# Probabilities of an attention kernel by pairs of key tiles, in instructions of 768 columns

## The chip, the cores and the metric

The kernel runs on one core of one Trainium2 chip. The metric is the time of one execution on the device, in microseconds. Three runs of the kernel before took 981.05, 981.09 and 982.55 us; their median is 981.09 us.

## The reference

Block-sparse attention of 4 batches x 8 heads, 768 positions, 64 columns a head, followed by a two-layer network on the 3072 tokens. All inputs are float32.

```
scores = q @ k^T / sqrt(64);  scores = -1e9 outside the block mask
attn   = softmax(scores);     attn_out = attn @ v
x = attn_out as [3072, 512];  h = x @ w_in                 # 512 -> 2048
g = h where h >= 1, 0 where h <= -1, else (h + 1)^2 / 4
out = g @ w_out                                            # 2048 -> 512
```

## The kernel before

**Heads.** A head is worked through in two halves of 384 queries (`HALF`), and a half in six key tiles of 128 (`T`), so a head has 12 steps. In a step, TensorE (PE) makes the scores of one key tile, keys on the 128 partitions and queries on the 384 columns, by two matmuls into a PSUM bank (`scores`, L318 and L319). ScalarE (ACT) takes the exponential out of the bank into SBUF (`expo`, L323, tile `pt`). The row maximum that the exponent needs is made ahead of the head: twelve matmuls (`max_mm`, L267), each read by a maximum on VectorE (DVE) (`max_red`, L272, tile `mc`). Scores, maxima and small jobs share one ring of three PSUM banks, `pa`.

**Split and whole heads.** Heads 0 to 9 (`WHOLE` names pairs of heads) use the float32 probabilities as they are. For the other 22 heads the probabilities are split into a rounded part and the rest, both in the format that TensorE takes faster: `p_hi` (L196 through the helper `rounded`, a cast on ScalarE, tile `ph`), `p_lo` (L331, a subtraction of two SBUF tiles on VectorE, tile `pl`). Two matmuls a key tile then multiply them with the values (`values`, L350 and L351, bank `po`). `pt`, `ph` and `pl` have three buffers each, of 384 columns.

**Sums of the softmax.** In split heads, GpSimd (POOL) adds up the six `pt` tiles of a half (`p_sum`, L338, five adds of 384 columns, tile `acc`). VectorE then sums over the partitions with a transposing reduction (`acc_sum`, L373, tile `psum`), and after the second head of a pair TensorE, VectorE and some DMAs finish the reciprocal (`sums` L378, `dens`, `recip`, `r_out`), with which `x_mul`, `x_hi` and `x_lo` make the network's input `x`.

**The network.** It runs one batch behind the heads, in slices of 128 hidden columns, one slice in three steps. TensorE makes the slice by twelve matmuls into the one bank `hp` (`l1`, L472 to L474). ScalarE takes relu and square (L478, L481), VectorE merges them with `hp` (`g_max`, L484, tile `r`) and so frees the bank for the next slice. Then follow a cast `gh` on ScalarE, a subtraction `gl` on VectorE (L493), and nine matmuls of 512 columns (`l2`, L500 to L502, banks `oa`). In the first half of batch 0's network, ScalarE and VectorE also convert `w_out` from float64 (L168 to L180).

**The order.** Every step is put into `plan` with a due time in steps (`at`), from tables of numbers (`P`, `PW`, `PA`, `PM`): a split tile's cast is due 1.22 steps behind its scores, its low part 1.349, its add 0.841, its values `lag` = 3.5. The network of batch b begins at step 96 (b + 1) + `DELAY`. The plan is sorted by due time and issued; a scheduler below it may still place an instruction ahead of others of its engine. Each engine then works strictly in its order, and waits where an input or a buffer isn't there.

Of the kernel before, what the change touches and what calls it, by code (L numbers as in the profile page):

```python
# [8 lines left out]
F32 = mybir.dt.float32  # L9
F32R = mybir.dt.float32r  # L10
# [3 lines left out]
ALU = mybir.AluOpType  # L14
# [23 lines left out]
def body(ctx, tc, qk_t, v, sampled_blocks, moe_w_in, moe_w_out, ind, cm, negd, ident, fold, out):  # L38
    nc = tc.nc
    pool = lambda name, bufs, **kw: ctx.enter_context(tc.tile_pool(name=name, bufs=bufs, **kw))  # L40
# [2 lines left out]
    tp = pool("tp", 1)  # L43
    qk = pool("qk", SETS)
    vp = pool("vp", 2)
    pp = pool("pp", 3)
    ac = pool("ac", 2)
    pr = pool("pr", 1)
    xp = pool("xp", 10)
# [1 line left out]
    op = pool("op", 1)  # L51
# [21 lines left out]
    def f(ap):  # L73
        return ap.bitcast(F32)
# [12 lines left out]
    def consts():  # L87
        M = slice(64, KM)
        for i in range(SETS):
            nc.gpsimd.memset(f(QA[i][64:128]), 0.0)  # L90
        nc.gpsimd.memset(VW[0][:, :, 64:128], 1.0)
        nc.gpsimd.memset(VW[1][:, :, 0:64], 1.0)
        nc.vector.memset(eps, 1e-9)
        nc.vector.memset(half_c, 0.5)
        sraw = cst.tile([128, NR, 2], I32, name="sraw")
        nc.sync.dma_start(out=sraw[M], in_=sampled_blocks.bitcast(I32).rearrange("a (r w) -> a r w", w=2))
        cmt = cst.tile([128, 2 * NB], F32, name="cmt")
        nc.sync.dma_start(out=cmt[M], in_=cm)
        ef = f(cv.tile([128, 512, 2], I32, name="raw", bufs=3).rearrange("p c w -> p (c w)"))[64:KA, 0:S]
        nc.sync.dma_start(out=ef, in_=ind)  # L100
        idf = pp.tile([128, HALF], F32, name="pt")[:, 0:128]
        nc.sync.dma_start(out=idf, in_=ident)
        nc.vector.tensor_copy(out=idr, in_=idf)
        nc.vector.tensor_copy(out=KAt[0][64:KA], in_=ef)
        nc.sync.dma_start(out=nd, in_=negd.rearrange("a (t p) -> a t p", t=T))
        nc.sync.dma_start(out=sel, in_=fold)
        for i in range(1, SETS):
            rounded(nc.gpsimd, KAt[i][64:KA], ef)
        sf = cst.tile([128, NR], F32, name="sf")
        nc.vector.tensor_copy(out=sf[M], in_=sraw[M, :, 0])  # L110
        al = cst.tile([128, NB], F32, name="al")
        nc.vector.tensor_copy(out=al[M], in_=cmt[M, 0:NB])
        for r in range(NR):
            nc.vector.scalar_tensor_tensor(
                out=al[M], in0=cmt[M, NB:2 * NB], scalar=sf[M, r:r + 1], in1=al[M],
                op0=ALU.is_equal, op1=ALU.max)
        mb = cst.tile([128, NB], F32R, name="mb")
        nc.vector.tensor_scalar(out=mb[M], in0=al[M], scalar1=-1.0, scalar2=BIG, op0=ALU.add, op1=ALU.mult)
        for hf in range(2):
            cs = slice(hf * HALF, (hf + 1) * HALF)  # L120
            pm = psa.tile([128, 512], F32, name="pa")
            nc.tensor.matmul(out=pm[0:NB, 0:HALF], lhsT=mb[M], rhs=KAt[0][64:KM, cs], start=True, stop=True)
            for i in range(SETS):
                (nc.scalar.copy if i else nc.vector.tensor_copy)(out=QA[i][64:KM, cs], in_=pm[0:NB, 0:HALF])
# [4 lines left out]
    def at(t, fn, *args):  # L129
        plan.append((t, fn, args))  # L130
# [59 lines left out]
    def rounded(eng, dst, src):  # L190
        if eng is nc.vector:
            eng.tensor_copy(out=dst, in_=src)
        elif eng is nc.gpsimd:
            eng.tensor_scalar(out=dst, in0=src, scalar1=1.0, scalar2=0.0, op0=ALU.mult, op1=ALU.add)
        else:
            eng.copy(out=dst, in_=src)  # L196

    def head(i, n0, b, h, pst):

        j, e = divmod(h, 2)  # L200
        wide = i < H
        whole = i // 2 in WHOLE
# [116 lines left out]
            nc.tensor.matmul(out=ps[:, 0:HALF], lhsT=st["KB"][:, ks], rhs=st["QB"][:, cs], start=False, stop=True)  # L319

        def expo(c):
            p = st["p", c] = pp.tile([128, HALF], F32, name=("pt", "ph", "pl")[c % 3] if wide else "pt")
            nc.scalar.activation(out=p, in_=st.pop(("ps", c))[:, 0:HALF], func=AF.Exp, scale=SCALE)  # L323
# [5 lines left out]
        def p_lo(c):
            pl = st["pl", c] = pp.tile([128, HALF], F32R, name="pl")  # L330
            (nc.gpsimd if i < 2 * H and c in PL1 else nc.vector).tensor_tensor(out=pl, in0=st["p", c], in1=f(st["ph", c]), op=ALU.subtract)  # L331

        def p_sum(hf, c):
            if c == 1:
                st["acc", hf] = ac.tile([128, HALF], F32, name="acc")
            if c:
                prev = st["p", 0] if c == 1 else st["acc", hf]
                nc.gpsimd.tensor_tensor(out=st["acc", hf], in0=prev, in1=st["p", c], op=ALU.add)  # L338

        def values(hf, c):  # L340
            if c == 0:
# [71 lines left out]
        for hf in range(2):  # L413
            for c in range(T):
                at(s, scores, hf, c)
                at(s + G["ex"], expo, c)
                if not whole:
                    at(s + G["ph"], p_hi, c)
                    at(s + G["pl"], p_lo, c)
                    at(s + G["ps"], p_sum, hf, c)  # L420
                at(s + G["lag"], values, hf, c)
                s += 1
            u = s - 1 + G["lag"]
            if whole:
                at(u + G["ow"], o_whole, hf)
            else:
                at(u + G["ot"], o_tmp)
                at(u + G["oa"], o_add, hf)
                at(u + G["al"], acc_sum, hf)
                if e:  # L430
                    at(u + G["su"], sums, hf)
                    at(u + G["de"], dens, hf)
            if e:
                y = u + (G["yw"] if whole else G["yy"])
                if whole:
                    at(y, r_in, hf)
# [144 lines left out]
PA = {'vw': 4.0, 'r1': 0.857, 'r2': 4.031, 'qs': 11.825, 'vs': 8.565, 'ld': 5, 'm0': 7.832, 'm1': 5.139, 'mr': 0.063, 'mc': 2.3, 'mt': 1.564, 'mw': 0.515, 'ex': 0.037, 'ph': 1.22, 'pl': 1.388, 'ps': 0.841, 'ow': 0.331, 'ot': 0.188, 'oa': 0.814, 'ah': 0.068, 'al': 0.538, 'su': 0.644, 'de': 1.414, 'yw': 0.799, 'yy': 1.698, 'xm': 0.186, 'xh': 1.352, 'xl': 3.084, 'lag': 3.5}  # L581
PM = {'gr': 0.039, 'gs': 0.186, 'gm': 0.351, 'gh': 0.912, 'gl': 1.158, 'l2': 1.494, 'l3': 0.158, 'l1': 0.131}
RINGS = {"s": ("oa0", "oa1", "hp"), "m": ("pa", "pa")}
DELAY = 3.672
EARLY = 0
SETS = 2
MANUAL = -999
# [56 lines left out]
```

## Time and profile before

| | |
|---|---|
| median of three runs | 981.09 us |
| profiled execution, its time | 980.94 us |
| its span, first to last instruction | 979.0 us |
| granted TensorE clock, mean | 0.995 |
| TensorE matmuls busy | 945.3 us, 97% |
| VectorE busy | 736.8 us, 75% |
| ScalarE busy | 646.3 us, 66% |
| GpSimd busy | 251.5 us, 26% |

A row of instructions in a timeline gives start, duration, engine, line and tiles, and in brackets the idle time of its engine before it and who ended it. A group's row gives the count, the busy time, the mean duration in ns, and the idle time before. In a row of a line's own view stand the shortest, the median and the longest duration. Matmuls overlap, so their rate is read from start to start. Heads 10 to 31, the split ones, run from about 205 to 835 us; after them the last batch's network runs alone.

### The profile page before, as it was taken

Reading aid. Unit: us, or ns where it says so; the run is one execution under the profiler, and the core shown is the slowest. Engines: PE = TensorE matmul, PEld = TensorE weight load, DVE = VectorE, ACT = ScalarE, POOL = GpSimd, SP = SyncE. Lnnn points to the kernel's source line nnn. Section 1 sums busy time; section 2 is a strip of 40 time slices with the busy share of each in tenths; the row PEclk is TensorE's granted clock in tenths of the full one; section 3 lists DMA queues with packets and bytes.
Section 4 is the critical chain, followed back from the end, with each engine's and each line's share of the span. In section 5 each row is a group of like instructions: output and inputs, shape, how many; then the busy total and the mean of one; then the engine's idle time right before and its main releaser. Section 6 shows DMA issues by size and latency. Waiting matters only on the chain.

```text
span 979.0 us, 14671 instructions
## 1 busy us (share of the span) xinstructions
PE 945.3 (97%) x4746; PEld 833.3 (85%) x4746; DVE 736.8 (75%) x1390; ACT 646.3 (66%) x1326; POOL 251.5 (26%) x229
## 2 busy tenths in 40 slices
PE   5898999999899999999999999999999999999998
PEld 3676677888789999998999899999999999899997
DVE  5897988779998888988888888888788885422222
ACT  4686787677677676767677667776767676433433
POOL 1000000013334443433434343433434343000000
PEclk9899999999999999999999999999999999999999
DMA  6756766754364544545556453646445442433442
GB/s 193 227 155 183 200 201 214 259 173 140 129 205 144 146 148 136 178 135 154 158 154 189 118 153 120 198 138 176 137 143 178 126 114 89 154 129 129 161 129 97
DMA packets 56216, 154.44 MB, mean 158 GB/s; under 512 B 9612, under 2 KB 17952, under 8 KB 56140
## 3 DMA queue, kind: packets, MB, share of 16 engines
q1 hardware_dynamic: 56100, 153.48, 52.0%
q8 instruction: 38, 0.62, 0.3%
q14 instruction: 38, 0.31, 0.1%
q10 hardware_dynamic: 40, 0.03, 0.0%
HBM read 100.92 MB, written 14.81 MB: 118 GB/s over the span
## 4 chain that ended last, share of the span: by engine, by line
PE 88%; DVE 5%; ACT 3%; DMA 2%; issue 2%; SPq 0%; ACTq 0%; DVEq 0%
PE oa L500 8%; PE oa L502 8%; PE oa L501 8%; PE hp L472 8%; PE hp L474 8%; PE hp L473 8%; PE pa L267 7%; PE pa L318 5%; PE pa L319 5%; PE po L350 5%; PE po L348 5%; PE po L351 4%; PE oa L348 3%; DVE mc L272 1%; PE oa L318 1%
## 5 line engine op out<-in xcount | busy, mean ns | idle before, releaser
L338 POOL TENSOR_TENSOR acc<-acc,pt 128x384 f32<-128x384 f32 x176 | 202.2, 1149 | 226.2 <-ACT pt L323 190.3
L272 DVE TENSOR_REDUCE mc<-pa 128x1 f32<-128x384 f32 x384 | 202.8, 548 | 24.1 <-PE pa L267 21.0
L196 ACT CAST ph<-pt 128x384 fp32r<-128x384 f32 x264 | 135.7, 514 | 88.2 <-PE po L350 84.5
L331 DVE TENSOR_TENSOR pl<-pt,ph 128x384 fp32r<-128x384 f32 x264 | 166.3, 630 | 35.6 <-ACT ph L196 34.9
L323 ACT ACTIVATE pt<-pa 128x384 f32<-128x384 f32 x288 | 140.6, 489 | 50.8 <-PE pa L319 42.0
L472 PE MATMUL hp<-x,wi 128*128 128x384 f32 x448 | 155.0, 346 | 2.9 <-DVE r L484 2.9
L500 PE MATMUL oa<-w,gh 128*128 128x512 f32 x384 | 153.6, 400 | 0.3 <-ACT gh L196 0.3
L502 PE MATMUL oa<-w,gl 128*128 128x512 f32 x384 | 151.4, 394 | 0.0
L473 PE MATMUL hp<-x,wi 128*128 128x384 f32 x448 | 151.4, 338 | 0.0
L474 PE MATMUL hp<-x,wi 128*128 128x384 f32 x448 | 151.2, 338 | 0.0
L501 PE MATMUL oa<-w,gh 128*128 128x512 f32 x384 | 150.8, 393 | 0.0
L267 PE MATMUL pa<-KA,QA 88*128 88x384 f32 x384 | 138.8, 381 | 5.3 <-DMA QA<-qkh 3.0
L338 POOL TENSOR_TENSOR acc<-pt 128x384 f32<-128x384 f32 x44 | 45.8, 1040 | 349.4 <-ACT pt L323 349.4
L484 DVE SCALAR_TENSOR_TENSOR r<-r,hp 128x384 f32<-128x384 f32 x112 | 61.7, 551 | 74.0 <-ACT r L481 73.6
L493 DVE TENSOR_TENSOR gl<-r,gh 128x384 fp32r<-128x384 f32 x128 | 83.7, 654 | 23.4 <-ACT gh L196 22.9
L478 ACT ACTIVATE r<-hp,half_c 128x384 f32<-128x384 f32 x112 | 65.1, 582 | 53.4 <-PE hp L474 50.3
L318 PE MATMUL pa<-QA,KA 102*128 102x384 f32 x288 | 99.3, 345 | 0.8 <-ACT pt L323 0.4
L319 PE MATMUL pa<-QB,KB 128*128 128x384 f32 x288 | 97.9, 340 | 0.0
L267 PEld LDWEIGHTS pa<-KA,QA 88*128 88x128 f32 x384 | 73.2, 192 | 27.8 <-DVE mc L272 6.7
L350 PE MATMUL po<-ph,vn 128*128 128x384 f32 x264 | 91.5, 347 | 2.3 <-DVE xun L360 1.9
L472 PEld LDWEIGHTS hp<-x,wi 128*128 128x128 f32 x448 | 84.5, 189 | 8.6 <-DVE r L484 4.2
L351 PE MATMUL po<-pl,vn 128*128 128x384 f32 x264 | 88.6, 336 | 0.0
(100 smaller groups left out, 1634.1 us busy)
## 6 DMA issues: line engine op xcount, KB each, us to landing
w<-wo_dram SPq DMA_DIRECT2D x112, 512.0 KB
qk<-in_qk_t_dram SPq DMA_DIRECT2D x32, 384.0 KB
raw<-in_moe_w_in_dram SPq DMA_DIRECT2D x16, 512.0 KB
raw<-in_moe_w_out_dram SPq DMA_DIRECT2D x16, 512.0 KB
wo_dram<-w SPq DMA_DIRECT2D x16, 512.0 KB
lv<-in_v_dram SPq DMA_DIRECT2D x32, 192.0 KB
KA<-qkh SPq DMA_DIRECT2D x32, 192.0 KB
QA<-qkh SPq DMA_DIRECT2D x32, 192.0 KB
```

The lines of the kernel that those rows point to most:

```text
L267: nc.tensor.matmul(out=pm[:, 0:HALF], lhsT=QAi[0:KM, t * 128:(t + 1) * 128], rhs=KAi[0:KM, kh * HALF:(kh + 1) * HALF], start=True, stop=True)
L272: nc.vector.reduce_max(out=st["mc"][:, t, kh:kh + 1], in_=st.pop(("pm", t, kh))[:, 0:HALF], axis=AX.X)
L318: nc.tensor.matmul(out=ps[:, 0:HALF], lhsT=KAi[0:KA, ks], rhs=QAi[0:KA, cs], start=True, stop=False)
L319: nc.tensor.matmul(out=ps[:, 0:HALF], lhsT=st["KB"][:, ks], rhs=st["QB"][:, cs], start=False, stop=True)
L331: (nc.gpsimd if i < 2 * H and c in PL1 else nc.vector).tensor_tensor(out=pl, in0=st["p", c], in1=f(st["ph", c]), op=ALU.subtract)
L338: nc.gpsimd.tensor_tensor(out=st["acc", hf], in0=prev, in1=st["p", c], op=ALU.add)
L472: nc.tensor.matmul(out=hv, lhsT=wi[:, j, 0, fs], rhs=x[:, 0], start=(j == 0), stop=False)
L473: nc.tensor.matmul(out=hv, lhsT=wi[:, j, 0, fs], rhs=x[:, 1], start=False, stop=False)
L474: nc.tensor.matmul(out=hv, lhsT=wi[:, j, 1, fs], rhs=x[:, 0], start=False, stop=(j == NP - 1))
L500: nc.tensor.matmul(out=o, lhsT=gh[:, ts], rhs=w[:, 0], start=(fi == 0), stop=False)
L501: nc.tensor.matmul(out=o, lhsT=gh[:, ts], rhs=w[:, 1], start=False, stop=False)
L502: nc.tensor.matmul(out=o, lhsT=gl[:, ts], rhs=w[:, 0], start=False, stop=(fi == NF - 1))
```

## The change

The probabilities of two neighbouring key tiles (a pair, `cp`) now lie in one tile of 2 x 384 columns. The exponentials still come one by one, each into its half. In split heads, one cast, one low part and one add work on 768 columns. The add of pair 1 takes pairs 0 and 1, that of pair 2 adds to it, and a last add of 384 columns folds the two halves of `acc` together. `ph` and `pl` have two buffers of 768 columns, `pt` three. The values of split heads stand 4.0 steps behind their scores instead of 3.5, so that they stand right ahead of the scores of four tiles later, and the network's begin moves by the same half step.

```diff
-    pp = pool("pp", 3)
+    pp = pool("pp", 2)
...
         def expo(c):
-            p = st["p", c] = pp.tile([128, HALF], F32, name=("pt", "ph", "pl")[c % 3] if wide else "pt")
+            cp, k = divmod(c, 2)
+            if k == 0:
+                st["pp", cp] = pp.tile([128, 2, HALF], F32, name=("pt", "ph", "pl")[cp] if wide else "pt",
+                                         bufs=2 if wide and cp else 3)
+            p = st["p", c] = st["pp", cp][:, k]
...
-        def p_hi(c):
-            ph = st["ph", c] = pp.tile([128, HALF], F32R, name="ph")
-            rounded(nc.vector if c in (PH1 if i < 2 * H else PH2) else nc.scalar, ph, st["p", c])
...
+        def p_hi(cp):
+            ph = st["php", cp] = pp.tile([128, 2, HALF], F32R, name="ph")
+            rounded(nc.scalar, ph, st["pp", cp])
+            st["ph", 2 * cp], st["ph", 2 * cp + 1] = ph[:, 0], ph[:, 1]
+
+        def p_lo(cp):
+            pl = pp.tile([128, 2, HALF], F32R, name="pl")
+            nc.vector.tensor_tensor(out=pl, in0=st["pp", cp], in1=f(st["php", cp]), op=ALU.subtract)
+            st["pl", 2 * cp], st["pl", 2 * cp + 1] = pl[:, 0], pl[:, 1]
+
+        def p_sum(hf, cp):
+            if cp == 0:
+                return
+            if cp == 1:
+                st["acc2", hf] = ac.tile([128, 2, HALF], F32, name="acc")
+            acc = st["acc2", hf]
+            nc.gpsimd.tensor_tensor(out=acc, in0=st["pp", 0] if cp == 1 else acc, in1=st["pp", cp], op=ALU.add)
+            if cp == 2:
+                nc.gpsimd.tensor_tensor(out=acc[:, 0], in0=acc[:, 0], in1=acc[:, 1], op=ALU.add)
+                st["acc", hf] = acc[:, 0]
...
-                if not whole:
-                    at(s + G["ph"], p_hi, c)
-                    at(s + G["pl"], p_lo, c)
-                    at(s + G["ps"], p_sum, hf, c)
-                at(s + G["lag"], values, hf, c)
+                if not whole and c % 2:
+                    at(s + G["ph"] - 0.5, p_hi, c // 2)
+                    at(s + G["pl"] - 0.5, p_lo, c // 2)
+                    at(s + G["ps"], p_sum, hf, c // 2)
+                at(s + (G["lag"] if whole else LAG), values, hf, c)
                 s += 1
-            u = s - 1 + G["lag"]
+            u = s - 1 + (G["lag"] if whole else LAG)
...
+LAG = 4.0
...
-DELAY = 3.672
+DELAY = 4.172
```

In the changed file these lines move down: the casts keep L196, the maxima L272, the scores L318 and L319, but the exponential is L327, the low part L336, the add L345, the fold L347, the values L360 and L361, psum L383, the first layer L482 to L484, r L494, gl L503, the second layer L510 to L512.

The instructions come to stand in another order. Three places are shown, two of VectorE and one of TensorE. The first is on VectorE, at the end of a head's second half, before (numbers behind a name tell buffers apart; r reads and frees `hp`, psum reads `acc`):

```order
L331 TENSOR_TENSOR pl_7345<-pt_7321,ph_7341 128x384
L484 SCALAR_TENSOR_TENSOR r_7343<-r_7343,hp_7292 128x384
L331 TENSOR_TENSOR pl_7367<-pt_7351,ph_7365 128x384
L373 TENSOR_REDUCE psum_7086<-acc_7231 128x12
L493 TENSOR_TENSOR gl_7369<-r_7343,gh_7363 128x384
L331 TENSOR_TENSOR pl_7389<-pt_7373,ph_7387 128x384
```

The same place on VectorE now:

```order
L336 TENSOR_TENSOR pl_6761<-pt_6720,ph_6757 128x768
L298 TENSOR_TENSOR QA0_113<-pa_6787,nd_109 6x768
L336 TENSOR_TENSOR pl_6816<-pt_6782,ph_6810 128x768
L383 TENSOR_REDUCE psum_6577<-acc_6759 128x12
L494 SCALAR_TENSOR_TENSOR r_6812<-r_6812,hp_6773 128x384
L503 TENSOR_TENSOR gl_6835<-r_6812,gh_6833 128x384
```

r stood ahead of the half's last low part and of psum; it now stands behind both. Of the 44 psums of the program, 21 stand so: those of all second halves from the third split head on, and that of the last head's first half. The second place is the end of a first half in every other head (heads 13, 15 and so on to 29, nine in all), while the next head's row maxima are made. VectorE had there before:

```order
L331 TENSOR_TENSOR pl_7157<-pt_7135,ph_7153 128x384
L272 TENSOR_REDUCE mc_7123<-pa_7147 128x1
L484 SCALAR_TENSOR_TENSOR r_7155<-r_7155,hp_7108 128x384
L272 TENSOR_REDUCE mc_7123<-pa_7159 128x1
L373 TENSOR_REDUCE psum_6924<-acc_7047 128x12
L272 TENSOR_REDUCE mc_7123<-pa_7171 128x1
```

and has now:

```order
L336 TENSOR_TENSOR pl_6650<-pt_6613,ph_6642 128x768
L272 TENSOR_REDUCE mc_6604<-pa_6646 128x1
L383 TENSOR_REDUCE psum_6435<-acc_6590 128x12
L494 SCALAR_TENSOR_TENSOR r_6644<-r_6644,hp_6607 128x384
L272 TENSOR_REDUCE mc_6604<-pa_6663 128x1
L272 TENSOR_REDUCE mc_6604<-pa_6673 128x1
```

Here r has come to stand behind psum, and two maxima behind both. The third place is TensorE's order at the end of the second half, up to the next slice's first matmul into `hp`; before, from the sixth row behind the half's last score matmul on:

```order
L500 MATMUL oa1_6190<-w_7112,gh_7274 128x512
L501 MATMUL oa1_6190<-w_7112,gh_7274 128x512
L502 MATMUL oa1_6190<-w_7112,gl_7285 128x512
L318 MATMUL pa_7357<-QA0_113,KA0_115 128x384
L319 MATMUL pa_7357<-QB_7105,KB_7104 128x384
L500 MATMUL oa2_6209<-w_7112,gh_7274 128x512
L501 MATMUL oa2_6209<-w_7112,gh_7274 128x512
L502 MATMUL oa2_6209<-w_7112,gl_7285 128x512
L350 MATMUL po_7287<-ph_7312,vn_6719 128x384
L351 MATMUL po_7287<-pl_7314,vn_6719 128x384
L472 MATMUL hp_7375<-x_2531,wi_119 128x384
```

and now the last twelve rows of the same stretch:

```order
L319 MATMUL pa_6822<-QB_6585,KB_6584 128x384
L510 MATMUL oa1_5772<-w_6611,gh_6751 128x512
L511 MATMUL oa1_5772<-w_6611,gh_6751 128x512
L512 MATMUL oa1_5772<-w_6611,gl_6765 128x512
L510 MATMUL oa2_5788<-w_6611,gh_6751 128x512
L511 MATMUL oa2_5788<-w_6611,gh_6751 128x512
L512 MATMUL oa2_5788<-w_6611,gl_6765 128x512
L360 MATMUL po_6767<-ph_6757,vn_6231 128x384
L361 MATMUL po_6767<-pl_6761,vn_6231 128x384
L318 MATMUL pa_6839<-QA0_113,KA0_115 128x384
L319 MATMUL pa_6839<-QB_6585,KB_6584 128x384
L482 MATMUL hp_6842<-x_2438,wi_119 128x384
```

The values now stand right ahead of the scores. Counted from the half's last score matmul (L319, itself counted) to L482 there are now 12 matmuls of 384 columns and 9 of 512: ahead of these rows stand that L319, the last three of `l1`, three of `l2`, two of the values and L318.

More of the change, by code (lines that the diff above doesn't have):

```diff
@@ L100, in consts @@
         nc.sync.dma_start(out=ef, in_=ind)
-        idf = pp.tile([128, HALF], F32, name="pt")[:, 0:128]
+        idf = pp.tile([128, 2, HALF], F32, name="pt", bufs=3)[:, 0, 0:128]
         nc.sync.dma_start(out=idf, in_=ident)
@@ L321, in expo @@
         def expo(c):
-            p = st["p", c] = pp.tile([128, HALF], F32, name=("pt", "ph", "pl")[c % 3] if wide else "pt")
-            nc.scalar.activation(out=p, in_=st.pop(("ps", c))[:, 0:HALF], func=AF.Exp, scale=SCALE)
-        def p_hi(c):
-            ph = st["ph", c] = pp.tile([128, HALF], F32R, name="ph")
-            rounded(nc.vector if c in (PH1 if i < 2 * H else PH2) else nc.scalar, ph, st["p", c])
[L329 to L338, printed above, removed]
+            cp, k = divmod(c, 2)
[3 more added lines that the diff above has]
+            p = st["p", c] = st["pp", cp][:, k]
+            nc.scalar.activation(out=p, in_=st.pop(("ps", c))[:, 0:HALF], func=AF.Exp, scale=SCALE)
+        def p_hi(cp):
[16 more added lines that the diff above has]
+                st["acc", hf] = acc[:, 0]
         def values(hf, c):
```

## The prediction

> **What bounds the kernel now.** I read the page's busy times first, then the stretches, then who made TensorE wait.
>
> ```profile
> span 979.0 us, 14671 instructions
> PE 945.3 (97%) x4746; PEld 833.3 (85%) x4746; DVE 736.8 (75%) x1390; ACT 646.3 (66%) x1326; POOL 251.5 (26%) x229
> ```
>
> The stretches from 200 to 800 us hold nearly all the heads that the change touches; columns are PE, PEld, DVE, ACT, POOL busy.
>
> ```profile
> 200.00:250.00 50.00, 46.67 (x236) 40.31 (x237) 44.50 (x76) 37.57 (x78) 15.96 (x14) 1.00 0.53 172
> 250.00:300.00 50.00, 46.07 (x238) 40.43 (x237) 48.99 (x90) 34.05 (x72) 18.58 (x16) 1.00 0.47 156
> 300.00:800.00 500.00, 497.55 (x2618) 458.27 (x2617) 419.33 (x785) 355.71 (x743) 198.96 (x178) 1.00 0.52 152
> ```
>
> PE idles 3.33 + 3.93 + 2.45 = 9.7 us in these 600. So PE sets the pace, and the most that any relief of the other engines can return here is 9.7 us; 7.3 of it lies in 200 to 300 us, where VectorE is 93.5% busy (84% later). The waits of PE in 200 to 800 us:
>
> ```profile
> PE hp L472 <- DVE r L484: 2.9, 2, 2.0
> PE po L350 <- DVE xun L360: 1.9, 3, 0.9
> PE pa L267 <- ACT pt L323: 1.2, 3, 0.5
> PE po L350 <- ACT xun L368: 0.4, 1, 0.4
> ```
>
> That PE is really at its rate is seen in the starts, not in the overlapping spans:
>
> ```profile
> 560.48 0.33 PE L350 MATMUL po<-ph,vn 128*128 128x384 f32 x1
> 560.65 0.34 PE L351 MATMUL po<-pl,vn 128*128 128x384 f32 x1
> 560.83 0.39 PE L500 MATMUL oa<-w,gh 128*128 128x512 f32 x1
> 561.06 0.40 PE L501 MATMUL oa<-w,gh 128*128 128x512 f32 x1
> 561.29 0.39 PE L502 MATMUL oa<-w,gl 128*128 128x512 f32 x1
> 561.52 0.34 PE L318 MATMUL pa<-QA,KA 102*128 102x384 f32 x1
> ```
>
> A 384-column matmul takes 0.175 us from start to start, a 512-column one 0.23. A PE stall is therefore lost for good, and the question is only which stalls go and which come.
>
> **The cheap parts.** Durations of the operations that are paired, and of two that already have 768 columns:
>
> ```profile
> L331 DVE TENSOR_TENSOR pl<-pt,ph x264: 482/551/1392, 209.5 to 832.6; 128x384 fp32r<-128x384 f32 x132
> L228 DVE TENSOR_TENSOR qk<-qk,qkh x32: 881/953/1766, 8.7 to 768.9; 128x768 f32<-128x768 f32 x32
> L196 ACT CAST ph<-pt 128x384 fp32r<-128x384 f32 x264 | 135.7, 514 | 88.2 <-PE po L350 84.5
> L196 ACT CAST qkh<-qk 128x768 fp32r<-128x768 f32 x32 | 26.7, 834 | 9.0 <-DMA qk<-in_qk_t_dram 8.5 <-DMA den<-s 0.3
> L338 POOL TENSOR_TENSOR acc<-acc,pt 128x384 f32<-128x384 f32 x176 | 202.2, 1149 | 226.2 <-ACT pt L323 190.3 <-DVE mc L272 28.9 <-DVE pl L331 5.7
> L194 POOL TENSOR_SCALAR KA<-raw 38x768 fp32r<-38x768 f32 x1 | 1.1, 1102 | 5.2 <-DMA raw<-in_ind_dram 5.2
> ```
>
> Of 264 low parts 132 are left: 132 x (2 x 0.551 - 0.953) = 20 us off VectorE. Of 264 casts likewise: 132 x (2 x 0.514 - 0.834) = 26 us off ScalarE, and the 84.5 us that ScalarE waited for PE to free a `ph` buffer go too, since the values that free it now precede the scores. Neither engine set the end, so this pays only where PE waited for them: the 1.2 and 0.4 us above, and perhaps half of the 2.9, together 3 us. The bounds of this gain are 0 and 9.7. No DMA is added, and SP's queue is passed by nothing new. The values' half step more is covered: a pair's low part ends about 3.8 us behind the start of its last score (below) and is wanted three steps behind it.
>
> **The dear part: what psum waits for.** In a half's end of the kernel before (second half of a head), in order of time:
>
> ```profile
> 383.99 0.34 PE L318 MATMUL pa<-QA,KA 102*128 102x384 f32 x1
> 384.17 0.34 PE L319 MATMUL pa<-QB,KB 128*128 128x384 f32 x1
> 384.67 0.48 ACT L323 ACTIVATE pt<-pa 128x384 f32<-128x384 f32 x1
> 385.29 1.02 POOL L338 TENSOR_TENSOR acc<-acc,pt 128x384 f32<-128x384 f32 x1 [1.32 <-ACT pt L323]
> 385.59 0.56 DVE L484 SCALAR_TENSOR_TENSOR r<-r,hp 128x384 f32<-128x384 f32 x1 [0.45 <-ACT r L481]
> 386.07 0.66 DVE L331 TENSOR_TENSOR pl<-pt,ph 128x384 fp32r<-128x384 f32 x1
> 386.08 0.34 PE L318 MATMUL pa<-QA,KA 102*128 102x384 f32 x1
> 386.65 0.56 DVE L373 TRANSPOSE_TENSOR_REDUCE psum<-acc 128x12 f32<-128x384 f32 x1
> 387.14 0.51 DVE L493 TENSOR_TENSOR gl<-r,gh 128x384 fp32r<-128x384 f32 x1
> ```
>
> Call the last score matmul's start s (384.17) and the last exponential's end E (385.15 = s + 0.98). GpSimd adds from E + 0.14 on, and psum runs at E + 1.5, behind r, which had freed `hp`. A step (386.08 - 383.99) is 2.1 us here. In the changed order r stands behind psum (the fences of the change), and psum now needs an add of 768 columns and a fold of 384. Two things price that. The first is that the two engines shut each other out:
>
> ```profile
> 352.80 1.33 POOL L338 TENSOR_TENSOR acc<-acc,pt 128x384 f32<-128x384 f32 x1 [1.51 <-ACT pt L323]
> 353.16 1.38 DVE L493 TENSOR_TENSOR gl<-r,gh 128x384 fp32r<-128x384 f32 x1
> 354.54 0.54 DVE L331 TENSOR_TENSOR pl<-pt,ph 128x384 fp32r<-128x384 f32 x1
> 354.61 2.22 POOL L338 TENSOR_TENSOR acc<-acc,pt 128x384 f32<-128x384 f32 x1 [0.49 <-ACT pt L323]
> 355.01 0.94 DVE L228 TENSOR_TENSOR qk<-qk,qkh 128x768 f32<-128x768 f32 x1
> ```
>
> The `gl` subtraction, begun inside a GpSimd add, ends 0.41 us behind that add's end (354.13) and takes 1.38 instead of 0.55. The second add, begun inside pl, waits through pl and qk, and ends 0.88 behind qk's end (355.95). Before, the cast and the wait ahead of it kept most low parts clear of the short add. Now add and cast start with the same E, the cast ends at about E + 0.87, and the low part meets an add that is still running.
>
> The second is the add's length. No row has it. Bounds: 1.10 us (the one GpSimd row of 768 columns, with one input) and 2 x 1.02 = 2.04. I take 1.90: of 1.02 us, 0.88 are left when the other engine lets go, so 0.88 grows with the columns and 0.14 does not. The Trainium skill (GPSIMD Engine Reference, 3.1) has a two-input GpSimd add at about 2.6 cycles an element, which makes an estimate of 0.83 us for 384 columns more, so 1.85; by it the sum below would be 1.5 us smaller.
>
> Working: add ends E + 0.14 + 1.90 = E + 2.04. The waiting low part goes first and ends 0.41 + 0.40 (its extra 384 columns, 0.953 - 0.551) later, E + 2.85; the fold ends 0.88 behind it, E + 3.73. From a GpSimd end to a psum that has nothing else to wait for:
>
> ```profile
> 426.11 1.02 POOL L338 TENSOR_TENSOR acc<-acc,pt 128x384 f32<-128x384 f32 x1 [1.70 <-DVE mc L272]
> 426.41 0.55 DVE L484 SCALAR_TENSOR_TENSOR r<-r,hp 128x384 f32<-128x384 f32 x1 [0.33 <-ACT r L481]
> 426.88 0.55 DVE L272 TENSOR_REDUCE mc<-pa 128x1 f32<-128x384 f32 x1
> 427.35 0.57 DVE L373 TRANSPOSE_TENSOR_REDUCE psum<-acc 128x12 f32<-128x384 f32 x1
> ```
>
> 0.22 us, so psum starts at E + 3.95. (If the fold goes first, the low part ends at E + 3.87 and psum starts at E + 3.8.) r starts 0.49 later and takes 0.56: it ends at E + 5.0 = s + 5.98. (Its own input comes from ScalarE's relu and square, which follow the cast there and wait for no GpSimd.) Behind r wait VectorE's `gl`, ScalarE's `gh` and one exponential, while PE stands still. PE wants `hp` for the next L482 after 12 matmuls of 384 columns and 9 of 512, s + 4.17: a stall of 1.8 us. Of 44 psums, 21 stand so (in the last, PE has only 3.65 us): 20 x 1.8 + 2.3 = 38.3 us. In 9 first halves, psum and r stand ahead of row maxima: mc starts 0.47 behind r and takes 0.55, so it ends at s + 6.44, and its bank is wanted again after 17 and 9 matmuls, s + 5.05: 9 x 1.4 = 12.6 us. Behind the other 14 psums no r or row maximum is wanted so soon; they cost PE nothing. Sum: 38.3 + 12.6 - 3 = +48 us. The profiled execution took 980.94 us, 0.15 under the median of 981.09, so **1029 us**.
>
> **The rivals.** *No shutting out*: the add takes 1.90, but the low part doesn't delay the fold. Then psum starts at E + 3.28; stalls 20 x 1.15 + 1.65 and 9 x 0.7, less 3: 1008 us. For it: GpSimd's spans are rough by the page's legend. Against it: the 1.38 above. *VectorE becomes the bound*: held low parts add about 1 us, twice a half, against 0.45 saved. In 200 to 300 us, with 93.5% busy, seven halves add some 8 us, and with the add at 2.04 (30 x 0.14 = 4): 1041 us. Against it: 84% busy from 300 us on. *A cheap add*: 1.10 us and no shutting out; psum starts at E + 2.48, stalls 20 x 0.35 + 0.9, none in the first halves: 986 us. Against it: 384 columns already take 1.02.
>
> *Faster*: psum is ready before it matters and the relief of VectorE and ScalarE shows; place: 200 to 300 us, price: most of the 7.3 us there, so 975 us. It decides where add and fold together take under 1.77 us (psum by E + 2.14, so that r ends by s + 4.17). Against it: the two rows give 1.10 + 1.02 = 2.12 at the least. The Trainium skill (VectorE: DVE Perf Modes, the section on the TRN2 errata) speaks for it: operations that read SBUF pay a fixed time per instruction, so wider tiles are better. The trace agrees on the price (0.953 against 2 x 0.551), but not on the place, since VectorE is not the bound.
>
> **How the numbers follow.** Chances: the forecast 0.62, no shutting out 0.14, VectorE bound 0.11, cheap add 0.05, faster 0.05, and 0.03 that stalls and relief cancel. What a measurement can tell from no change is about 0.2%, 2 us (the three runs spread over 1.5). The range goes from 1003, under the second case, to 1045, over the third. Faster 0.05, same 0.03, slower 0.92.
>
> **What would show it.** Right: POOL rows of 768 columns near 1.9 us; psum (L383) at E + 3.5 or later with VectorE idle or held before it; `PE hp L482 <- DVE r L494` at the head of PE's waits with some 20 of about 1.8 us, then `PE pa L267 <- DVE mc L272`; casts and low parts of 0.83 and from 0.95 to 2 us; PE busy in 300 to 800 us about 92% instead of 99.5%. Wrong: those waits of PE missing, r ahead of psum in time, or a GpSimd add near 1.1 us.

## The result, and the profile after

The changed kernel takes 1035.88 us (median of 6 runs, 1034.88 to 1037.04), beside 981.07 us for the kernel before (6 runs): a ratio of 1.0561, interval 1.0544 to 1.0579. It is slower, by 55 us where 48 were forecast, and the time lies inside the forecast's range. The profiled execution took 1034.88 us. Its page begins with the span and the busy times; the third line is the chain of waits by engine, where POOL did not appear before.

```profile
span 1033.1 us, 13733 instructions
PE 963.0 (93%) x4746; PEld 831.2 (80%) x4746; DVE 776.5 (75%) x1258; ACT 628.6 (61%) x1194; POOL 240.3 (23%) x141
PE 64%; DVE 14%; POOL 10%; ACT 6%; issue 3%; DMA 2%; POOLq 0%; SPq 0%; ACTq 0%; DVEq 0%
```

The stretches, with the same columns as in the prediction (PE, PEld, DVE, ACT, POOL busy, then PEclk):

```profile
200.00:250.00 50.00, 45.36 (x231) 39.15 (x229) 44.59 (x71) 36.70 (x70) 14.12 (x7) 1.00 0.61 191
250.00:300.00 50.00, 47.70 (x235) 42.27 (x236) 47.56 (x80) 32.80 (x60) 16.99 (x9) 0.97 0.42 136
300.00:800.00 500.00, 470.03 (x2392) 416.45 (x2391) 415.34 (x614) 311.32 (x581) 173.93 (x99) 1.00 0.47 141
```

From 300 to 800 us PE now idles 30.0 us where it idled 2.45, and VectorE is no busier in this stretch than before (415 against 419 us). Over the whole execution VectorE's busy time rose from 736.8 to 776.5 us, though it has 132 low parts fewer: an operation that GpSimd holds counts as busy while it stands still, as shown below. Four of PE's waits over the whole execution, in the changed file's line numbers:

```profile
PE hp L482 <- DVE r L494: 26.6, 22, 1.8
PE pa L267 <- DVE mc L272: 6.4, 16, 0.8
PE po L360 <- DVE xun L370: 5.8, 4, 2.8
PE pa L267 <- ACT pt L327: 1.2, 4, 0.3
```

The first line stood at 2.9 us in 2 waits before. One of its 22, in order of time: the half's last score matmul starts at 455.00, its exponential (L327) ends at E = 455.87.

```profile
455.00 0.34 PE L319 MATMUL pa<-QB,KB 128*128 128x384 f32 x1
455.38 0.49 ACT L327 ACTIVATE pt<-pa 128x384 f32<-128x384 f32 x1 [1.83 <-PE pa L319]
456.01 1.85 POOL L345 TENSOR_TENSOR acc<-acc,pt 128x768 f32<-128x768 f32 x1 [2.93 <-ACT pt L327]
456.77 1.90 DVE L336 TENSOR_TENSOR pl<-pt,ph 128x768 fp32r<-128x768 f32 x1 [0.83 <-ACT ph L196]
457.94 1.60 POOL L347 TENSOR_TENSOR acc<-acc 128x384 f32<-128x384 f32 x1
459.01 0.34 PE L319 MATMUL pa<-QB,KB 128*128 128x384 f32 x1
459.57 0.58 DVE L383 TRANSPOSE_TENSOR_REDUCE psum<-acc 128x12 f32<-128x384 f32 x1 [0.90 <-POOL acc L347]
460.08 0.52 DVE L494 SCALAR_TENSOR_TENSOR r<-r,hp 128x384 f32<-128x384 f32 x1
460.65 0.44 PE L482 MATMUL hp<-x,wi 128*128 128x384 f32 x1 [1.29 <-DVE r L494]
460.93 0.34 PE L483 MATMUL hp<-x,wi 128*128 128x384 f32 x1
```

Read it from the bottom up. L482 stood still until r had freed `hp`; r stood behind psum; VectorE idled 0.90 us ahead of psum until the fold was done; the fold took 1.60 us beside a low part of 1.90 us, which in turn lay under the pair add of 1.85. The gap of 1.29 understates the loss, since a matmul's span overlaps the next: from start to start L319 to L482 took 1.64 us instead of 0.175, and L482 to L483 0.28. So a stall costs about 1.57 us, of which 0.28 is in no wait.

Counted that way over all PE rows behind 200 us (what lies between two starts beyond 0.175 or 0.23 us, by what ended the wait), PE lost 71.7 us after and 18.3 before. Of the 53.4 between them, r has 29.1 (32.5 against 3.4), the row maxima 13.0 (14.8 against 1.8), the sum `xun` 4.2, the small read of the sums' bank (rc) 3.5, and many short gaps the rest.

Not all of this hangs on psum. Of the row maxima's 14.8 us, 6.9 lie in the nine first halves that the prediction named, 0.77 each. Most of the other waits for row maxima, all nine for rc and three of the four for `xun` come behind a VectorE operation with two SBUF inputs that stands still beside one of GpSimd's pair adds. One of them, with the pair add first:

```profile
357.37 1.82 POOL L345 TENSOR_TENSOR acc<-pt 128x768 f32<-128x768 f32 x1 [6.72 <-ACT pt L327]
357.49 1.72 DVE L276 TENSOR_TENSOR mr<-mc 128x6 fp32r<-128x6 f32 x1
359.73 0.45 PE L360 MATMUL po<-ph,vn 128*128 128x384 f32 x1 [1.72 <-DVE xun L370]
```

`mr`, a small operation on the row maxima, took at most 0.17 us before. Here it ends at 359.21, just behind the add (359.19); `xun` follows it, and PE waits 1.72 us for `xun`. No psum stands there. Ahead of rc it is mostly `gl`, with up to 1.91 us where its median is 0.56.

### The profile page after: what moved, and what is told of

Read it like the earlier page. It is cut to its first block, busy times and chain, and to the rows that moved or that the text cites. A ratio compares the mean times of both kernels' runs of the same rounds, so it can differ in the third digit from the quotient of the medians.

```text
span 1033.1 us, 13733 instructions
## 1 busy us (share of the span) xinstructions
PE 963.0 (93%) x4746; PEld 831.2 (80%) x4746; DVE 776.5 (75%) x1258; ACT 628.6 (61%) x1194; POOL 240.3 (23%) x141
## 4 chain that ended last, share of the span: by engine, by line
PE 64%; DVE 14%; POOL 10%; ACT 6%; issue 3%; DMA 2%; POOLq 0%; SPq 0%; ACTq 0%; DVEq 0%
PE hp L482 7%; PE hp L484 6%; PE hp L483 6%; PE pa L267 6%; POOL acc L345 5%; PE oa L510 5%; PE oa L512 5%; PE oa L511 5%; POOL acc L347 5%; PE po L358 4%; DVE mc L272 3%; PE po L360 3%; PE pa L319 3%; PE pa L318 3%; PE po L361 3%
## 5 line engine op out<-in xcount | busy, mean ns | idle before, releaser
L327 ACT ACTIVATE pt<-pa 128x384 f32<-128x384 f32 x288 | 140.5, 489 | 159.0 <-PE pa L319 157.4
L272 DVE TENSOR_REDUCE mc<-pa 128x1 f32<-128x384 f32 x384 | 200.1, 547 | 23.3 <-PE pa L267 17.8
L345 POOL TENSOR_TENSOR acc<-pt 128x768 f32<-128x768 f32 x44 | 83.5, 1898 | 509.4 <-ACT pt L327 509.4
L482 PE MATMUL hp<-x,wi 128*128 128x384 f32 x448 | 156.8, 350 | 26.6 <-DVE r L494 26.6
L336 DVE TENSOR_TENSOR pl<-pt,ph 128x768 fp32r<-128x768 f32 x132 | 158.6, 1201 | 26.3 <-ACT ph L196 23.5
L510 PE MATMUL oa<-w,gh 128*128 128x512 f32 x384 | 154.8, 403 | 0.3 <-ACT gh L196 0.3
L267 PE MATMUL pa<-KA,QA 88*128 88x384 f32 x384 | 141.9, 390 | 14.0 <-DVE mc L272 6.4
L483 PE MATMUL hp<-x,wi 128*128 128x384 f32 x448 | 151.6, 338 | 0.0
L512 PE MATMUL oa<-w,gl 128*128 128x512 f32 x384 | 151.5, 395 | 0.0
L484 PE MATMUL hp<-x,wi 128*128 128x384 f32 x448 | 151.4, 338 | 0.0
L503 DVE TENSOR_TENSOR gl<-r,gh 128x384 fp32r<-128x384 f32 x128 | 97.0, 758 | 37.5 <-ACT gh L196 37.1
L196 ACT CAST gh<-r 128x384 fp32r<-128x384 f32 x128 | 65.4, 511 | 94.6 <-DVE r L494 94.4
L482 PEld LDWEIGHTS hp<-x,wi 128*128 128x128 f32 x448 | 84.9, 189 | 37.4 <-DVE r L494 34.0
L494 DVE SCALAR_TENSOR_TENSOR r<-r,hp 128x384 f32<-128x384 f32 x112 | 60.5, 540 | 71.6 <-ACT r L491 71.6
L345 POOL TENSOR_TENSOR acc<-acc,pt 128x768 f32<-128x768 f32 x44 | 83.4, 1895 | 126.9 <-ACT pt L327 126.9
L196 ACT CAST ph<-pt 128x768 fp32r<-128x768 f32 x132 | 110.4, 837 | 2.8
L318 PE MATMUL pa<-QA,KA 102*128 102x384 f32 x288 | 101.0, 351 | 1.3 <-DVE mc L272 0.8
L319 PE MATMUL pa<-QB,KB 128*128 128x384 f32 x288 | 98.5, 342 | 0.0
L360 PE MATMUL po<-ph,vn 128*128 128x384 f32 x264 | 91.5, 347 | 5.9 <-DVE xun L370 5.8
L361 PE MATMUL po<-pl,vn 128*128 128x384 f32 x264 | 89.1, 338 | 0.0
```

Source lines behind the costliest of these rows:

```text
L267: nc.tensor.matmul(out=pm[:, 0:HALF], lhsT=QAi[0:KM, t * 128:(t + 1) * 128], rhs=KAi[0:KM, kh * HALF:(kh + 1) * HALF], start=True, stop=True)
L272: nc.vector.reduce_max(out=st["mc"][:, t, kh:kh + 1], in_=st.pop(("pm", t, kh))[:, 0:HALF], axis=AX.X)
L336: nc.vector.tensor_tensor(out=pl, in0=st["pp", cp], in1=f(st["php", cp]), op=ALU.subtract)
L345: nc.gpsimd.tensor_tensor(out=acc, in0=st["pp", 0] if cp == 1 else acc, in1=st["pp", cp], op=ALU.add)
L482: nc.tensor.matmul(out=hv, lhsT=wi[:, j, 0, fs], rhs=x[:, 0], start=(j == 0), stop=False)
L483: nc.tensor.matmul(out=hv, lhsT=wi[:, j, 0, fs], rhs=x[:, 1], start=False, stop=False)
```

## The experiments

Four theories were tested. **A**: the loss is VectorE's wait in psum for GpSimd's long sums, with r and the row maxima queued behind it. **Rival 1**: the half step by itself, which puts r behind psum. **Rival 2**: the low parts of 768 columns, which stand still (are held) while a GpSimd add runs. **Rival 3**: VectorE is full. Each run's ratio is to the kernel before on the same chip.

| run | us, median | ratio, interval |
|---|---|---|
| e1_lag_only | 985.73 | 1.0052 (1.0037 to 1.0067) |
| e2_psum_later | 1000.15 | 1.0197 (1.0166 to 1.0227) |
| e3_short_adds | 984.07 | 1.0030 (1.0013 to 1.0046) |
| e4_one_more | 1100.38 | 1.1236 (1.1185 to 1.1287) |
| e5_pair_casts | 976.78 | 0.9953 (0.9935 to 0.9972) |
| e6_no_fold | 1023.77 | 1.0447 (1.0414 to 1.0479) |
| e7_no_half_step | 989.34 | 1.0089 (1.0063 to 1.0115) |
| e8_no_last_low | 1040.01 | 1.0611 (1.0582 to 1.0641) |
| e9_both_moves | 985.56 | 1.0042 (1.0024 to 1.0060) |
| e10_casts_psum_later | 975.62 | 0.9939 (0.9919 to 0.9960) |

**e1_lag_only: the half step alone**, in the kernel before.

```diff
-                at(s + G["lag"], values, hf, c)
+                at(s + (G["lag"] if whole else LAG), values, hf, c)
...
-            u = s - 1 + G["lag"]
+            u = s - 1 + (G["lag"] if whole else LAG)
...
+LAG = 4.0
...
-DELAY = 3.672
+DELAY = 4.172
```

> The kernel before, with only the half step of the change: the values of the heads of pairs 5 and up stand four steps behind the scores instead of three and a half, and the second stage starts 0.5 step later. Casts, low parts and adds stay at 384 columns. In VectorE's order r now stands behind psum at the ends of second halves, as in the changed kernel. Theory A (the loss is VectorE's wait in psum for the long pair adds and the fold on GpSimd): psum waits for one add of 1.02 us here and costs next to nothing, 978 to 985 us. Rival 1 (the half step itself, which puts r and the row maxima behind psum, is the cost): about 1030 us. Rival 2 (the low parts of 768 columns, held by GpSimd, are the cost) and rival 3 (VectorE is full): 978 to 985 too, since neither is in this kernel.

985.73 us: 4.6 us more than before and 50 less than the changed kernel. On VectorE r stands directly behind psum here as well (first line GpSimd's last add, then VectorE's queue, at the end of a second half):

```profile
445.63 1.02 POOL L338 TENSOR_TENSOR acc<-acc,pt 128x384 f32<-128x384 f32 x1 [1.04 <-DVE pl L331]
```

```profile
446.69 0.58 DVE L373 TRANSPOSE_TENSOR_REDUCE psum<-acc 128x12 f32<-128x384 f32 x1 [1.11 <-POOL acc L338]
447.19 0.52 DVE L484 SCALAR_TENSOR_TENSOR r<-r,hp 128x384 f32<-128x384 f32 x1
```

psum begins 1.06 us behind the add's start instead of 3.56 (459.57 - 456.01), so r is done 2.5 us earlier, and PE shows no stall there. Being behind psum costs nothing as long as psum is early. Rival 1 falls as the main cause. Where its 4.6 us lie was not settled; its profiled execution has two stretches of half the clock behind 200 us (the last section tells of such stretches), where the kernel before has none.

**e3_short_adds: the changed kernel with the adds of before**, five of 384 columns for each half, without fold.

```diff
-        def p_sum(hf, cp):
...
+        def p_sum(hf, c):
+            if c == 1:
+                st["acc", hf] = ac.tile([128, HALF], F32, name="acc")
+            if c:
+                prev = st["p", 0] if c == 1 else st["acc", hf]
+                nc.gpsimd.tensor_tensor(out=st["acc", hf], in0=prev, in1=st["p", c], op=ALU.add)
```

> The changed kernel with GpSimd's sums as before: five adds of 384 columns for each half, no pair adds and no fold; casts and low parts stay at 768 columns, values stay four steps behind. Theory A: psum waits for one add of 1.02 us, the loss goes and the cheap parts (26 us less on ScalarE, 20 us less on VectorE) stand alone, 972 to 988 us. Rival 1 (the half step): about 1035 us. Rival 2 (low parts of 768 columns held by GpSimd): the five adds hold the low parts as the pair adds did, 1010 to 1036 us. Rival 3 (VectorE is full): about 1030 us.

984.07 us, inside theory A's numbers: of the 55 us 52 are gone, with all the pair casts, pair low parts and the half step still in. All three rivals wanted 1010 or more. VectorE even idles longer ahead of psum than in the changed kernel (35.8 us in 21 waits against 22.9 in 30), so that idle time itself is not the loss. What counts is when psum begins: about 1.2 us behind E at the end of a second half (E = 441.14, psum at 442.33) instead of 3.70. PE hardly waits for r:

```profile
PE hp L479 <- DVE r L491: 1.4, 2, 1.1
```

**e5_pair_casts: the cheap parts alone**, e3 with the lag and the due times of before.

```diff
-LAG = 4.0
+LAG = 3.5
...
-DELAY = 4.172
+DELAY = 3.672
```

> Casts and low parts by pairs (768 columns) as in the changed kernel; the adds as before (five of 384 columns for each half), and no half step: values three and a half steps behind the scores, second stage due as before. So the cheap parts alone. Theory A with what the lag-only run (985.7 us) and the short-adds run (984.1 us) showed, namely that the half step costs some 4 us and the loss lies in the long adds: 977 to 983 us, TensorE busy throughout, so nothing is gained from ScalarE's 26 us. Rival 1 (the half step was needed, so that a pair's low part is ready in time for its values): over 990 us.

976.78 us, 3.7 us faster than before (980.50 on that chip). Casts and low parts by pairs gain what the prediction gave them, and no half step is needed for it. Engines from 300 to 800 us, PE first:

```profile
300.00:800.00 500.00, 499.75 (x2627) 460.05 (x2626) 403.98 (x680) 334.10 (x636) 200.18 (x179) 1.00 0.53 151
```

VectorE and ScalarE have 15 and 22 us less to do than before in this stretch, but PE is busy for all but 0.25 us of it: nothing more can come of them.

**e7_no_half_step: the whole change but its half step** (LAG and DELAY as in e5, pair adds and fold kept).

> The whole change but its half step: casts, low parts and adds by pairs with the fold, values three and a half steps behind the scores and the second stage due as before. On VectorE r and its low part gl then stand ahead of psum at the ends of second halves; at the ends of first halves psum still stands among the row maxima. Theory A (the loss is what stands behind a late psum): the waits for r go, those for the row maxima stay in part, 985 to 1005 us. Rival 2 (held low parts) and rival 3 (VectorE is full): the same work in another order, 1025 to 1036 us. Rival 1 (the half step by itself): about 981 us.

989.34 us. On VectorE r and gl now stand ahead of psum at the ends of second halves, and PE's wait for r is as short as before; the row maxima behind the first halves' psum stay:

```profile
PE pa L318 <- DVE mc L272: 5.4, 5, 1.1
...
PE hp L482 <- DVE r L494: 3.0, 3, 1.9
```

So the half step alone costs 0.5%, the rest of the change without it 0.9%, and both together 5.6%. Neither part holds the loss; it needs a late psum and r behind it.

**e2_psum_later: the changed kernel with psum moved** behind r and xun on VectorE; all sizes stay (`st["oadd"]` is the sum `xun` of L370).

```diff
-            nc.vector.tensor_reduce(out=pst["ps", hf][:, e], in_=st["acc", hf].rearrange("p (a j) -> p a j", j=32),
-                                    axis=AX.X, op=ALU.add, apply_transpose=True)
+            with tc.issue_after(st["oadd"].ins):
+                nc.vector.tensor_reduce(out=pst["ps", hf][:, e], in_=st["acc", hf].rearrange("p (a j) -> p a j", j=32),
+                                        axis=AX.X, op=ALU.add, apply_transpose=True)
...
-                at(u + G["al"], acc_sum, hf)
+                at(u + G["oa"] + 0.03, acc_sum, hf)
...
-                    at(u + G["su"], sums, hf)
+                    at(u + G["oa"] + 0.06, sums, hf)
```

> The changed kernel with psum moved: on VectorE it stands behind r and the xun sum of its half, about one and a half steps later, and no longer waits for the fold. All instructions and their sizes stay. Theory A: the waits of PE's hp for r (about 31 us) and of pa for the row maxima (about 15 us) mostly go, 985 to 1000 us. Rival 1 (the half step): about 1035 us. Rival 2 (held low parts) and rival 3 (VectorE is full): no instruction is shorter, 1025 to 1036 us.

1000.15 us, 0.15 over theory A's range: another place for psum on VectorE (and for the small matmul that reads it) returns 36 of the 55 us, about what was counted above for r and the nine first halves (29.1 and 6.9). The wait for r shrinks, and from 300 to 800 us VectorE is busier than in the changed kernel (432.56 against 415.34 us), not less busy, which is against rival 3:

```profile
PE hp L483 <- DVE r L495: 6.3, 11, 3.0
```

**e9_both_moves and e10_casts_psum_later.** e9 is e2 with LAG 3.5 and DELAY 3.672; e10 is e5 with e2's edit.

> The whole change with its pair adds and fold, but without the half step and with psum behind r and the xun sum of its half, in first and second halves alike, so that nothing of VectorE stands behind the fold before the fold is done. Adds, low parts and casts keep their sizes; the low parts are still held by GpSimd. Theory A (GpSimd's longer sums cost only what VectorE waits for in psum): 976 to 985 us. Rival 2 (held low parts) and rival 3 (VectorE is full): no better than the run without the half step, 989 us or more.

> The best version so far (casts and low parts by pairs, adds of 384 columns, no half step: 976.8 us) with psum behind r and the xun sum of its half. TensorE waits there for r 3 us and for other work of VectorE about 3 us after 200 us. Theory A: psum waits for next to nothing there already, so moving it gains at most 3 us: 973 to 978 us. Rival (psum still delays r and the row maxima through its own 0.58 us): 970 us or less.

e9 took 985.56 us, 0.6 over theory A's range; e10 975.62. They differ only in GpSimd's sums (two pair adds and a fold against five short adds), and psum waits in neither. VectorE's 300 to 800 us and its operations with two SBUF inputs, e9:

```profile
300.00:800.00 500.00, 498.38 (x2591) 452.16 (x2590) 457.33 (x667) 332.27 (x630) 191.50 (x107) 1.00 0.52 150
```

```profile
L336 DVE TENSOR_TENSOR pl<-pt,ph 128x768 fp32r<-128x768 f32 x132 | 164.4, 1245 | 15.8 <-ACT ph L196 15.7
L504 DVE TENSOR_TENSOR gl<-r,gh 128x384 fp32r<-128x384 f32 x128 | 130.9, 1023 | 22.3 <-ACT gh L196 22.2
```

and e10:

```profile
L336 DVE TENSOR_TENSOR pl<-pt,ph 128x768 fp32r<-128x768 f32 x132 | 133.4, 1011 | 39.4 <-ACT ph L196 37.6
L501 DVE TENSOR_TENSOR gl<-r,gh 128x384 fp32r<-128x384 f32 x128 | 87.4, 683 | 21.8 <-ACT gh L196 21.5
```

With the long adds the two groups take 74.5 us more ((164.4 + 130.9) - (133.4 + 87.4)), for the same instructions. VectorE at 91% (457.33 of 500) is nearer to full than in the changed kernel, and yet the kernel is 50 us faster. Rival 3 falls, and rival 2 is left with what separates e9 from e10, 10 us. (e9 differs from e2 in the half step alone, and that costs 15 us here where it cost 4.6 in e1; why was not settled.) The rival in e10's expectation falls too: psum's own length does not matter there. e10 is 0.6% faster than the kernel before; from e5 it cannot be told apart.

**e4_one_more: a longer wait.** One more add of 384 columns (zeros) behind each fold.

```diff
                 nc.gpsimd.tensor_tensor(out=acc[:, 0], in0=acc[:, 0], in1=acc[:, 1], op=ALU.add)
+                nc.gpsimd.tensor_tensor(out=acc[:, 0], in0=acc[:, 0], in1=zero, op=ALU.add)
```

> The changed kernel with one more add of 384 columns on GpSimd behind each fold (zeros are added to the sum), so that psum waits about 1.0 us longer, 42 times in all for the split heads; VectorE's, ScalarE's and TensorE's instructions stay. Theory A: each of the 20 or so waits for r and of the waits for the row maxima grows by up to 1.0 us, 25 to 40 us more than the changed kernel: 1060 to 1076 us. Rival 1 (the half step): 1035 to 1040 us. Rival 2 (held low parts): only the low part beside the added add is held longer, 0 to 15 us more. Rival 3 (VectorE is full by its busy time): 1035 to 1040 us.

1100.38 us, 24 over theory A's range. The waits answer as theory A has them, from 26.6 to 49.0 us for as many waits for r, 22, so 1.02 us more each, about the length of the added add (1.05):

```profile
PE hp L485 <- DVE r L497: 49.0, 22, 2.9
PE pa L269 <- DVE mc L274: 18.3, 18, 1.9
```

With the row maxima's 11.9 that is 34.3 us of 64.6 (the spans, 1097.7 and 1033.1). Another 27 are in PE's busy time, 990.1 us for the same 4746 matmuls, and there the granted clock (the first number behind the busy times) is down from 1.00 to 0.96:

```profile
300.00:800.00 500.00, 444.74 (x2170) 395.82 (x2169) 380.91 (x557) 281.79 (x526) 188.05 (x120) 0.96 0.43 127
```

The section on the hardware shows where. The expectation had left this out.

**e6_no_fold: a shorter wait.** psum reduces both halves of the pair sum, and the small matmul of the sums runs twice.

```diff
-            if cp == 2:
-                nc.gpsimd.tensor_tensor(out=acc[:, 0], in0=acc[:, 0], in1=acc[:, 1], op=ALU.add)
-                st["acc", hf] = acc[:, 0]
+            st["acc", hf] = acc
...
-                pst["ps", hf] = pr.tile([128, 2, 12], F32, name="psum", bufs=3)
+                pst["ps", hf] = pr.tile([128, 2, 2, 12], F32, name="psum", bufs=3)
```

> The changed kernel without the fold: psum reduces both halves of the pair sum (768 columns, some 0.4 us longer than 384), and the matmul of the sums runs twice, once for each half, into one bank. The pair adds stay at 768 columns, the half step stays. Theory A: psum begins behind the pair add, at E+2.0 instead of E+3.7 (E is the end of the half's last exp), r ends at about E+4.3 instead of E+4.7 if the low part stands between them, at E+3.4 if not; the wait for r shrinks from 1.3 to between 0 and 0.85 us each: 995 to 1020 us. Rival 1 (the half step) and rival 3 (VectorE is full, which now has 42 x 0.4 us more to do): 1035 to 1050 us.

1023.77 us, 4 over theory A's range. Where the order is the one of the fence above, psum begins behind the add, the low part follows, then r:

```profile
452.42 0.98 DVE L381 TRANSPOSE_TENSOR_REDUCE psum<-acc 128x24 f32<-128x768 f32 x1 [1.96 <-POOL acc L345]
453.32 0.92 DVE L336 TENSOR_TENSOR pl<-pt,ph 128x768 fp32r<-128x768 f32 x1
454.16 0.55 DVE L493 SCALAR_TENSOR_TENSOR r<-r,hp 128x384 f32<-128x384 f32 x1
```

The L481 behind it waited 0.89 us, the upper case of the expectation (0.85). The low part, no longer beside a running GpSimd operation, takes 0.92 us instead of 1.90. The expectation counted the waits for r alone; those for the row maxima and others that stay were not traced one by one.

**e8_no_last_low: nothing beside the last add.** The last pair's low part is left out, and its values use the one before.

```diff
+            if cp == 2:
+                pl = st["plp"]
+            else:
+                pl = st["plp"] = pp.tile([128, 2, HALF], F32R, name="pl")
+                nc.vector.tensor_tensor(out=pl, in0=st["pp", cp], in1=f(st["php", cp]), op=ALU.subtract)
-            pl = pp.tile([128, 2, HALF], F32R, name="pl")
-            nc.vector.tensor_tensor(out=pl, in0=st["pp", cp], in1=f(st["php", cp]), op=ALU.subtract)
```

> The changed kernel without the low part of each half's last pair (left out: the values matmuls of that pair read the low part of the pair before), so that nothing of VectorE reads two tiles of SBUF beside the last pair add and the fold. Adds, fold, psum and the half step stay. If VectorE's low part and GpSimd's add shut each other out (fold 1.60 us beside the low part), the fold takes about 1.0 us here, psum begins at about E+3.1 instead of E+3.7 and each wait for r or a row maximum shrinks by about 0.6 us: 1008 to 1020 us. If they don't (the fold takes 1.6 us by itself): the fold and psum stay where they are, 1030 to 1036 us.

1040.01 us: the time is neither theory's. At the end of a second half all is as expected of the shutting out (E = 462.32):

```profile
462.46 1.85 POOL L348 TENSOR_TENSOR acc<-acc,pt 128x768 f32<-128x768 f32 x1 [2.94 <-ACT pt L327]
464.39 1.01 POOL L350 TENSOR_TENSOR acc<-acc 128x384 f32<-128x384 f32 x1
465.44 0.58 DVE L386 TRANSPOSE_TENSOR_REDUCE psum<-acc 128x12 f32<-128x384 f32 x1 [3.05 <-POOL acc L350]
465.95 0.52 DVE L497 SCALAR_TENSOR_TENSOR r<-r,hp 128x384 f32<-128x384 f32 x1
466.52 0.44 PE L485 MATMUL hp<-x,wi 128*128 128x384 f32 x1 [0.71 <-DVE r L497]
```

The fold takes 1.01 instead of 1.60, psum begins at E + 3.12, and the stall is 0.71 instead of 1.29. But the scheduler answered the missing instruction with another order: in the first halves psum came to stand ahead of more row maxima (in one it began at E + 3.12 where it had begun, harmlessly, at E + 7.95), and the waits for these grew:

```profile
PE pa L267 <- DVE mc L272: 18.7, 39, 1.0
```

So the mutual exclusion is shown in the place, and what it costs the whole kernel is not shown by this run.

## Why the prediction was right

The mechanism is the forecast one, psum in VectorE's queue late behind GpSimd, with r and the row maxima behind it: e3 (shorter sums), e2 and e7 (another order) and e4 (longer sums) each move it as it should move. Point by point:

- *PE sets the pace, relief of the others pays little.* Right. e5 gained 3.7 us, the prediction 3. ScalarE's cast group is 110.4 us instead of 135.7 (25 less, forecast 26), and its idle time ahead of the casts fell from 88.2 to 2.8. In the changed kernel itself the gain did not come: its waits for `pt` are still 1.2 us. VectorE's 20 us came in e5 (15 from 300 to 800 us) but not in the changed kernel, whose VectorE is busy 39.7 us longer than before: held operations (`mr` and `gl` above all, and many low parts) took more than the 20 us. The two groups of the changed kernel, casts and low parts:

```profile
L196 ACT CAST ph<-pt 128x768 fp32r<-128x768 f32 x132 | 110.4, 837 | 2.8
```

```profile
L336 DVE TENSOR_TENSOR pl<-pt,ph x132: 881/949/2217, 210.2 to 883.2; 128x768 fp32r<-128x768 f32 x132
```

The low part's median is 0.949 us as forecast (0.953), its mean 1.20 (158.6 us for the 132), so the 132 save 7.7 us of the 166.3 that the 264 took.

- *The pair add, 1.90 us.* It took 1.85 (the median). The Trainium skill (GPSIMD Engine Reference, 3.1), with some 2.6 cycles an element, had made the estimate 1.85, and the trace agrees: 384 columns more cost 0.83 us over the 1.02.
- *Add, low part and fold, one behind the other.* Ends forecast at E + 2.04, 2.85 and 3.73, measured at E + 1.99, 2.80 and 3.67 in the place shown. Low part and fold each wait for the other engine, as supposed; e8 takes one away and the other shortens.
- *psum 0.22 us behind the fold.* Wrong: 0.03 (459.54 to 459.57). In the row that this was read from (psum at 427.35) VectorE was busy with a row maximum until then, so the row showed VectorE's queue, not the way from GpSimd to VectorE.
- *The stall for r, 20 x 1.8 + 2.3 = 38.3 us.* This is the mis-sized term. The places are right (22 waits against 21), the size is 29.1 more than before: 1.57 us by starts in the place shown and about 1.4 in others (a wait of 1.11 instead of 1.29), since psum came 0.25 earlier (3.70 against 3.95) and E is s + 0.87, not s + 0.98.
- *First halves, 9 x 1.4 = 12.6 us.* Also mis-sized: the nine cost 6.9 us. That all waits for row maxima together rose by 13.0 is a coincidence, since most of the others stand behind held operations.
- *Not in the prediction:* what held operations of VectorE cost PE outside psum's chain. The sum `xun` and the read rc (4.2 + 3.5 us) and the other row maxima wait behind them. The prediction saw the holding but charged it to psum and, in a rival, to VectorE's busy time.
- *The total, +48 against +55.* Near in part by luck. The two terms of psum's chain were forecast at 50.9 us and came to 36.0; the waits behind held operations, which it had at nothing, and short gaps made up the difference, and the gain of 3 did not come.
- *The rivals.* No shutting out falls in e8 (its sum, 20 x 1.15 + 1.65 + 9 x 0.7 - 3, gives 1009 us, not 1008). VectorE as the bound falls in e9 (seven halves at its prices, 2 us held against 0.45 saved, make 10.9 us; how they become 8 is not shown). The cheap add falls by its duration. *Faster* had the right effect without its condition: the Trainium skill (VectorE: DVE Perf Modes, the section on the TRN2 errata) prefers wider tiles, and wider low parts and casts alone are faster, e5's 0.47%, once nothing waits for a long sum.

## What to carry to other kernels

An engine works its queue in order: before an operation on another engine is made longer, ask what stands behind the one that waits for it, not only who reads its result. Two edits that each cost under 1% cost 5.6% together here, because one made an operand late and the other put urgent work behind its reader; another place for the reader returns most of it (e9 stays 0.4% slower than before), and pairing only the casts and low parts, without the long sums, gains 0.5%. A long GpSimd add also holds VectorE operations beside it, and what stands behind those waits too. And a wait's own length understates a TensorE stall: count from start to start.

## What the runs showed of the hardware

Longer stalls of PE cost more than themselves. In e4 a wait of 2.37 us is followed, 1.3 us later, by matmuls at 0.32 us from start to start instead of 0.175:

```profile
477.64 0.44 PE L485 MATMUL hp<-x,wi 128*128 128x384 f32 x1 [2.37 <-DVE r L497]
...
478.78 0.36 PE L485 MATMUL hp<-x,wi 128*128 128x384 f32 x1
478.96 0.51 PE L486 MATMUL hp<-x,wi 128*128 128x384 f32 x1
479.26 0.53 PE L487 MATMUL hp<-x,wi 128*128 128x384 f32 x1
479.58 0.53 PE L363 MATMUL po<-ph,vn 128*128 128x384 f32 x1
```

The slow stretch is one of half the granted clock, 3.41 us long. The first row, the 3.41 us ahead of it, holds most of the wait; columns are as in the stretches above:

```profile
475.55:478.96 3.41, 1.32 (x8) 1.32 (x9) 1.81 (x4) 1.31 (x3) 0.98 (x1) 1.00 0.99 252
478.96:482.37 3.41, 3.41 (x12) 3.32 (x12) 1.66 (x3) 1.64 (x4) 0.00 (x0) 0.50 0.58 136
```

e4's profile has 18 such stretches from 200 to 955 us, each of 3.41 us; they begin whole multiples of 3.41 us apart. At half speed each loses at most 1.7 us, together 31, which is of the size of the 27 us above. From 300 to 800 us of the changed kernel, with stalls of 1.1 to 1.3 us in the same places, the granted clock stayed at 1.00; its 0.97 from 250 to 300 us is one such stretch, at 250.90, behind a wait of 2.79 us for `xun`. The Trainium skill (TensorE: Matmul & The Clock Gate, HAM oscillation) asks for no idle gaps of PE over about 3.4 us; here 2.37 us were enough, and 1.77 us in e1 (half the clock from 248.48), so by these traces the limit is lower. The length of one wait does not decide alone: in e8 such a stretch (from 388.68) follows two waits, of 0.98 and 0.65 us. What the traces suggest is PE's idle time in the 3.41 us just ahead: in e4 all 18 follow 1.9 us of it or more, and 1.8 us or less was never followed by one. No sharp limit came out, since in e1 1.5 us were enough. No run was made to test this.
